# Attention, FFN and routed experts on one core: another order of the opening, and the first two tiles' mask laid into PSUM by TensorE

## The chip, the cores and the metric

The kernel runs on one core of a Trainium2 chip. The metric is the device time of one launch in microseconds (us). Engines: TensorE (PE), VectorE (DVE), ScalarE (ACT), GpSimd (POOL) and SyncE (SP), which issues most of the DMAs.

## The reference

Inputs are float32; two weight matrices of the FFN come as float64. Three stages follow each other:

```python
# 1: attention, batch 4, 8 heads, head_dim 64; 512 local and 32 global positions
k_all = np.concatenate([k_g, k_l], axis=2); v_all = np.concatenate([v_g, v_l], axis=2)
out_g = sm(scale * q_g @ k_all.T) @ v_all                  # global rows see all
mask = np.abs(pos[:, None] - pos[None, :]) <= 32           # local rows: a band, and the globals
s_ll = np.where(mask, scale * q_l @ k_l.T, -1000000000.0)
out_l = sm(np.concatenate([scale * q_l @ k_g.T, s_ll], -1)) @ np.concatenate([v_g, v_l], axis=2)
x = concatenate([out_g, out_l], axis=2)                    # as (4 * 544, 512) tokens
# 2: FFN 512 -> 2048 -> 512
h = x @ w_in; r = np.maximum(h, 0.0); x = (r * r) @ w_out
# 3: routed experts: 8 of 512 -> 1024 -> 512
do_compute = x @ w_skip > 0
e_idx = np.argmax(xc @ w_gate, axis=1)
out[do_compute] = xc + gate_w * (np.maximum(xc @ w1[e], 0.0) @ w2[e])
```

## The kernel before

Tokens are worked in 16 local tiles of 128 and one tile of globals; two tiles make a block of 256 for the FFN. Program order is fixed by hand (a manual schedule): each engine runs its instructions in the order in which the Python code emits them, and `SEQ`, a string of tokens that `do` (L1204 and after) walks through, sets that order up to the third FFN block. `EVEN`, `ODD` and `TAIL` do the same for the rest.

The tokens that matter here: `Lk..`, `Lq.`, `Lg.` issue loads of keys, queries and globals; `P00`, `P01`, `P0`, `P1` copy a loaded tile into the layout that the transposes want (L291, L310); `V` issues loads of the windows of values (`load_v`, L353); `W` fetches one weight of the FFN (L209), `A` takes one step of assembling weights (`assemble`, L237). `0G`, `00` to `03`, `0q` and `1q` transpose globals, keys and queries through PSUM and evict them (L316 to L343). `0a`, `0b`, `1a`, `1b` each advance the attention of tile 0, 1, 2 or 3 by one step, `F0`, `E0`, `H0`, `I0` the FFN of block 0 by one.

A weight arrives as float64, 128x512 numbers in 512 KB, and is turned into float32 by three kinds of steps: ACT rescales the high words (`rebase`, L219), DVE shifts the low words (`lower`, L223), joins the high words to them (`upper`, L227) and sets the sign (`sign`, L233). One `A` does `rebase` and `lower` of the next weight and `upper` and `sign` of this one; 32 weights are made so, in the order: four of w_in, four of w_out, and so on. Block 0 uses the first 24 of them as plain float32: its unit f needs the w_in weights 8*(f//4) to 8*(f//4)+3 for `first(f)` (h, L697) and one w_out weight for `second(f)` (acc, L723). Between them ACT takes the relu (g, L704) and ACT or DVE the square (gh, L743 or L741).

Attention of one tile (`attention`, L392) has six steps. (1) PE computes scores of 8 heads into two PSUM tiles, group 0 and 1 (L413); DVE adds the mask of group 0 (L426), takes the maximum (L430) and scales it (L431); ACT takes four exponents, one per head (L433). (2) The same for group 1. (3), (4) PE transposes the weights of a group (ptr, L442), ACT copies them to SBUF (pT, L444). (5) PE multiplies with the values (po, L451), DVE normalizes (xt, L461). (6) PE transposes the result (xtr, L280) and ACT copies it to the FFN's input (L468, `whole`). Transposes share two PSUM buffers, tag "tr", with group 1 of the scores of every tile but tile 1.

SP issues DMAs in the order of the code, each waiting for the one eight places ahead. Values lie in the opening in stages `v0` to `v3` (seven windows), later in six buffers `vr0` to `vr5`; each window is 96 local rows and, beneath them, the 32 global rows.

## Time and profile before

| | us |
|---|---|
| median of 3 runs (711.06 to 715.13) | 712.71 |
| the profiled execution | 706.99 |
| its span, first to last instruction | 705.3 |
| PE busy in the span | 680.9 (97%) |
| DVE / ACT / POOL busy | 395.0 / 365.2 / 163.9 |
| mean granted TensorE clock | 0.985 |

The profile is of one execution; the span is what its instructions cover, and 1.7 us lie around it. Busy shares are means over the whole program, so a stage is read in windows and in the timeline of each engine. In the timeline a row gives start, duration, engine, line, operation, what it writes and reads, shapes, the count of merged instructions, and in brackets how long the engine sat idle before it and what released it. The granted clock is a share of 2.4 GHz: 1.00 is 2.4 GHz, 0.50 is 1.2 GHz.

### The profile page before, as it was taken

How to read it: one execution, taken by the hardware profiler on the slowest of the kernel's cores; microseconds unless marked ns; L12 is line 12 of the kernel's file. 1: busy time of each engine (PE TensorE's matmuls, PEld its weight loads, DVE VectorE, ACT ScalarE, POOL GpSimd, SP SyncE). 2: the span in 40 equal slices, each digit the busy share in tenths (PEclk: the TensorE clock that was granted, in tenths of full speed). 3: DMA queues.
4: the chain of work that ended last, by engine and by line, in shares of the span. 5: the costliest groups of instructions: out<-in, count | busy, mean ns of one | idle time of the engine just before them, and what ended most of it. 6: DMA issues, size and time to landing. Idle time of an engine off the chain costs nothing. (4 is left out here: it accounts for less than half of the span.)

```text
span 705.3 us, 18628 instructions
## 1 busy us (share of the span) xinstructions
PE 680.9 (97%) x7621; PEld 573.8 (81%) x7621; DVE 395.0 (56%) x1072; ACT 365.2 (52%) x939; POOL 163.9 (23%) x206
## 2 busy tenths in 40 slices
PE   6689998999999999999999999999999999999996
PEld 4566667889888988888888998888887887898875
DVE  1889964872655165275426526544238733915985
ACT  5767568675535555453465445344434514614863
POOL 6000053453212212211211221122220432401311
PEclk8799999999999999999999999999999999999998
DMA  9999643064063401306340120410026689952930
GB/s 276 247 303 288 235 117 80 2 161 96 2 147 90 111 32 36 84 2 147 99 102 32 45 67 2 162 62 1 32 87 194 213 268 346 372 218 82 359 123 22
DMA packets 118841, 94.20 MB, mean 134 GB/s; under 512 B 84805, under 2 KB 91973, under 8 KB 118740
## 3 DMA queue, kind: packets, MB, share of 16 engines
q1 hardware_dynamic: 108352, 71.01, 35.9%
q10 hardware_dynamic: 8292, 15.48, 6.8%
q0 software_dynamic: 2096, 6.36, 2.7%
q8 instruction: 64, 1.05, 0.6%
q14 instruction: 37, 0.30, 0.2%
HBM read 80.57 MB, written 12.66 MB: 132 GB/s over the span
## 5 line engine op out<-in xcount | busy, mean ns | idle before, releaser
L184 POOL TENSOR_TENSOR gl<-g,gh 128x256 fp32r<-128x256 f32 x107 | 79.5, 743 | 302.8 <-ACT gh L183 142.3
L700 PE MATMUL h<-xh,w_in 128*128 128x256 f32 x464 | 135.1, 291 | 0.7 <-ACT xh L183 0.7
L701 PE MATMUL h<-xl,w_in 128*128 128x256 f32 x464 | 129.7, 280 | 0.3 <-DVE xl L184 0.3
L702 PE MATMUL h<-xh,w_in 128*128 128x256 f32 x464 | 129.8, 280 | 0.0
L725 PE MATMUL acc<-w_out,gh 128*128 128x512 f32 x232 | 97.6, 421 | 1.5 <-ACT gh L183 1.5
L727 PE MATMUL acc<-w_out,gl 128*128 128x512 f32 x232 | 91.9, 396 | 0.2
L726 PE MATMUL acc<-w_out,gh 128*128 128x512 f32 x232 | 91.7, 395 | 0.0
L700 PEld LDWEIGHTS h<-xh,w_in 128*128 128x128 f32 x464 | 87.2, 188 | 4.2 <-ACT xh L183 0.9
L701 PEld LDWEIGHTS h<-xl,w_in 128*128 128x128 f32 x464 | 87.3, 188 | 2.6 <-DVE xl L184 0.5
L704 ACT ACTIVATE g<-h 128x256 f32<-128x256 f32 x128 | 48.7, 381 | 77.0 <-PE h L702 43.7
L702 PEld LDWEIGHTS h<-xh,w_in 128*128 128x128 f32 x464 | 87.2, 188 | 0.0
L433 ACT ACTIVATE sm<-sm,mx 128x128 f32<-128x128 f32 x120 | 46.7, 390 | 49.5 <-DVE mx L431 49.5
L741 DVE TENSOR_TENSOR g<-h,g 128x256 f32<-128x256 f32 x53 | 22.2, 419 | 85.5 <-ACT g L704 85.5
L183 ACT CAST gh<-g 128x256 fp32r<-128x256 f32 x116 | 47.1, 406 | 42.2 <-DVE g L741 40.1
L727 PEld LDWEIGHTS acc<-w_out,gl 128*128 128x128 f32 x232 | 43.6, 188 | 11.9 <-POOL gl L184 1.3
L725 PEld LDWEIGHTS acc<-w_out,gh 128*128 128x128 f32 x232 | 43.6, 188 | 8.5 <-ACT gh L183 1.9
L726 PEld LDWEIGHTS acc<-w_out,gh 128*128 128x128 f32 x232 | 43.8, 189 | 5.7
L426 DVE TENSOR_TENSOR sm<-sc,mask 128x512 f32<-128x512 f32 x30 | 20.6, 687 | 23.3 <-PE sc L413 22.6
L255 POOL TENSOR_TENSOR w_in<-st_raw_in,w_in 128x512 fp32r<-128x512 f32 x10 | 13.0, 1308 | 80.0 <-ACT w_in L251 80.0
L743 ACT ACTIVATE g<-g 128x256 f32<-128x256 f32 x63 | 26.3, 417 | 5.0 <-ACT g L704 2.5
L413 PEld LDWEIGHTS sc<-kT,qT 64*32 64x32 f32 x2048 | 25.2, 110 | 4.3 <-issue 3.5
L413 PE MATMUL sc<-kT,qT 64*32 64x32 f32 (+1 forms) x2048 | 27.4, 230 | 0.0
(718 smaller groups left out, 1461.9 us busy)
## 6 DMA issues: line engine op xcount, KB each, us to landing
st_e<-in_moe_w_dram SPq DMA_DIRECT2D x46, 512.0 KB, 7.5
vr<-in_v_l_dram SPq DMA_DIRECT2D x49, 192.0 KB, 4.3
st_raw_in<-in_moe_w_in_dram SPq DMA_DIRECT2D x16, 512.0 KB, 6.6
st_raw_out<-in_moe_w_out_dram SPq DMA_DIRECT2D x16, 512.0 KB, 8.2
st_e<-in_moe_w_dram ACTq DMA_DIRECT2D x12, 512.0 KB, 5.5
x2d<-x ACTq DMA_DIRECT2D x19, 256.5 KB, 3.7
st_gv<-in_v_l_dram SPq DMA_DIRECT2D x8, 512.0 KB, 4.5
out_dram<-x ACTq DMA_DIRECT2D x16, 256.0 KB, 3.5
```

The lines of the kernel that those rows point to most:

```text
L183: nc.scalar.copy(hi, src)
L184: (lo_engine or nc.vector).tensor_tensor(out=lo, in0=src, in1=hi.bitcast(F32), op=ALU.subtract)
L413: nc.tensor.matmul(scs[g][SEG * i:SEG * (i + 1), p, cols], lhsT=q[rows, p, SEG * i:SEG * (i + 1)], rhs=kT[b][rows, p, keys], start=True, s ...
L433: nc.scalar.activation(sm[:, hh, :], sm[:, hh, :], AF.Exp, bias=mx[:, hh:hh + 1], scale=SCALE, accum_out=osum[:, 2 * hh + g:2 * hh + g + 1],)
L700: nc.tensor.matmul(h, lhsT=wh, rhs=xh[:, k, :], start=(k == 0), stop=False)
L701: nc.tensor.matmul(h, lhsT=wh, rhs=xl[:, k, :], start=False, stop=False)
L702: nc.tensor.matmul(h, lhsT=wl, rhs=xh[:, k, :], start=False, stop=(k == KD - 1))
L704: nc.scalar.activation(g, h, AF.Relu)
L725: nc.tensor.matmul(acc[z], lhsT=gh[:, c], rhs=wh, start=first_one, stop=False)
L726: nc.tensor.matmul(acc[z], lhsT=gh[:, c], rhs=wl, start=False, stop=False)
L727: nc.tensor.matmul(acc[z], lhsT=gl[:, c], rhs=wh, start=False, stop=last_one)
L743: nc.scalar.activation(square, g, AF.Square)
```

## The change

Five things. (1) `SEQ` has another beginning. (2) For tiles 0 and 1 TensorE lays the mask into the score tiles with one bf16 product per group (`ident_b`, an identity, is the stationary operand, and the mask, broadcast over four heads, the moving one), the scores accumulate upon it, DVE takes the maximum straight from PSUM, and ACT's exponents read PSUM; masks of all tiles are bf16 now. (3) One key copy, the evictions of key pairs 2 and 3, and half of the first query block's go from ACT to DVE. (4) The global rows of the values are loaded once; POOL copies them into the other six windows of the opening and into the six buffers of batch 0. (5) The load of the second query block comes later, two fetches of weights earlier.

```diff
 SEQ = """
-    Lk01 Lk00 P00 Lg0 0G P01 Lq0 P0 00 02 V Lq1 01 0q W 03 W A W W 0a A V V 0a A W W A 0a 0b 0a 0b A 0b W P1 W 0a A
-    0b A V 0a W 0b V A 1q W W A 0b V 1a W W F0 A W E0 1a W W A W V 1a A F0 W 1a I0 A 1b L9 1a H0 V A A W V E0 W 1a
+    Lk01 Lk00 P00 Lg0 0G P01 Lq0 P0 00 02 W W V 01 0q W W 03 A 0a V 0a A Lq1 0a 0a A V W 0b 0b V 0a W A W P1 0a 0b
+    0b W A W V 0b 0b W V 1q W F0 A 1a W A E0 A 1a A W V F0 A 1a W W I0 A 1a A 1b W W W L9 1a H0 V A A A W V E0 W 1a
     X0 H0 A A E0 H0 W H0 A H0 W 1b E0 Lg1 A A W W A E0 1b W H0 A 1b E0 A H0 A E0 Lv00 A W W W 1g A I0 C 1b A 1g I0 W
...
-        m = const.tile([P, P], F32, name=f"mask{kind}")
+        m = const.tile([P, P], BF16, name=f"mask{kind}")
...
+    ident_b = const.tile([P, P], BF16, name="ident_b")
+    nc.gpsimd.tensor_copy(ident_b, ident)
...
-            puts[f"{b}{z}"] = lambda: nc.scalar.copy(kin[b, z], t.rearrange("p h j d -> p j h d"))
+            copy = nc.vector.tensor_copy if z else nc.scalar.copy
+            puts[f"{b}{z}"] = lambda: copy(kin[b, z], t.rearrange("p h j d -> p j h d"))
...
-        nc.scalar.copy(kT[b][:, p, 0:SL].rearrange("p (q j) -> p j q", j=TPB), tr)
+        copy = nc.vector.tensor_copy if b == 0 and p > 1 else nc.scalar.copy
+        copy(kT[b][:, p, 0:SL].rearrange("p (q j) -> p j q", j=TPB), tr)
...
-                nc.scalar.copy(qT[j][:, 2 * z + a, :].rearrange("p (q i) -> p i q", i=2), tr[:, a])
+                copy = nc.vector.tensor_copy if j == 0 and z else nc.scalar.copy
+                copy(qT[j][:, 2 * z + a, :].rearrange("p (q i) -> p i q", i=2), tr[:, a])
...
+                if len(opening) == 1:
+                    nc.sync.dma_start(heads(w[WIN:P]), v_g[b].rearrange("h s d -> s h d"))
+                else:
+                    nc.gpsimd.tensor_copy(w[WIN:P], opening[0][WIN:P])
                 nc.sync.dma_start(heads(w[0:WIN]), v_l[b, :, w0:w0 + WIN, :].rearrange("h s d -> s h d"))
-                nc.sync.dma_start(heads(w[WIN:P]), v_g[b].rearrange("h s d -> s h d"))
...
-                nc.sync.dma_start(heads(windows[k][WIN:P]), v_g[b].rearrange("h s d -> s h d"))
+                if b == 0:
+                    nc.gpsimd.tensor_copy(windows[k][WIN:P], opening[-1][WIN:P])
+                else:
+                    nc.sync.dma_start(heads(windows[k][WIN:P]), v_g[b].rearrange("h s d -> s h d"))
...
+        masked = t < 2
+        if masked:
+            for sc in scs:
+                nc.tensor.matmul(
+                    sc, lhsT=ident_b, rhs=mask.unsqueeze(1).to_broadcast([P, 4, P]), start=True, stop=False,
+                )
...
-                            start=True, stop=True,
+                            start=not masked, stop=not masked or (globals_ and p == NPAIR - 1),
...
-            nc.vector.tensor_tensor(
-                out=sm, in0=scs[g], in1=mask.unsqueeze(1).to_broadcast([P, 4, P]), op=ALU.add,
-            )
+            if masked:
+                src = scs[g]
+            else:
+                src = sm
+                nc.vector.tensor_tensor(
+                    out=sm, in0=scs[g], in1=mask.unsqueeze(1).to_broadcast([P, 4, P]), op=ALU.add,
+                )
             mx = sb("mx", 2, [P, 4], f"mx{t}_{g}")
-            nc.vector.tensor_reduce(out=mx, in_=sm, op=ALU.max, axis=AX.X)
+            nc.vector.tensor_reduce(out=mx, in_=src, op=ALU.max, axis=AX.X)
...
-                    sm[:, hh, :], sm[:, hh, :], AF.Exp, bias=mx[:, hh:hh + 1], scale=SCALE,
+                    sm[:, hh, :], src[:, hh, :], AF.Exp, bias=mx[:, hh:hh + 1], scale=SCALE,
```

Lines of the changed program lie a few to 21 further down: the scores are L430 there, the mask's product L420, maximum and scaling L451 and L452, exponents L454.

What that does to the order is seen best on three engines. A name such as sm1_0 is of tile 1, group 0; the last number is the buffer's. First DVE, from the scores of tile 0 on, before:

```order
L426 TENSOR_TENSOR sm0_0_339<-sc0_0_273,mask0_75 128x512
L430 TENSOR_REDUCE mx0_0_341<-sm0_0_339 128x4
L431 TENSOR_SCALAR mx0_0_341<-mx0_0_341 128x4
L227 SCALAR_TENSOR_TENSOR st_raw_in_0_0_256<-st_raw_in_0_0_256 128x512
L223 TENSOR_SCALAR st_raw_in_1_0_264<-st_raw_in_1_0_264 128x512
L233 SCALAR_TENSOR_TENSOR st_raw_in_0_0_256<-st_raw_in_0_0_256 128x512
L426 TENSOR_TENSOR sm0_1_362<-sc0_1_274,mask0_75 128x512
L430 TENSOR_REDUCE mx0_1_364<-sm0_1_362 128x4
L431 TENSOR_SCALAR mx0_1_364<-mx0_1_364 128x4
```

and now, from the same place:

```order
L451 TENSOR_REDUCE mx0_0_341<-sc0_0_272 128x4
L452 TENSOR_SCALAR mx0_0_341<-mx0_0_341 128x4
L451 TENSOR_REDUCE mx0_1_354<-sc0_1_273 128x4
L452 TENSOR_SCALAR mx0_1_354<-mx0_1_354 128x4
L229 SCALAR_TENSOR_TENSOR st_raw_in_0_0_231<-st_raw_in_0_0_231 128x512
L225 TENSOR_SCALAR st_raw_in_1_0_233<-st_raw_in_1_0_233 128x512
L235 SCALAR_TENSOR_TENSOR st_raw_in_0_0_231<-st_raw_in_0_0_231 128x512
L229 SCALAR_TENSOR_TENSOR st_raw_in_1_0_233<-st_raw_in_1_0_233 128x512
L225 TENSOR_SCALAR st_raw_in_2_0_259<-st_raw_in_2_0_259 128x512
```

Between tile 0's two maxima no weight step stands any more, and the adds are gone; the weight steps come behind.

Second PE, around tile 1's scores (po is the product with the values). Before, behind the scores:

```order
L413 MATMUL sc1_1_392<-kT0_198,qT0_241 32x32
L442 MATMUL ptr0_1_466<-ident_70,sm0_1_362 128x128 x4
L442 MATMUL ptr1_0_485<-ident_70,st_sm1_457 128x128 x4
L451 MATMUL po0_497<-st_v0_229,pT0_0_388 32x64 x3
L451 MATMUL po0_497<-st_v1_354,pT0_0_388 32x64
```

and now, ahead of them:

```order
L463 MATMUL ptr0_0_368<-ident_70,sm0_0_340 128x128 x4
L463 MATMUL ptr0_1_375<-ident_70,sm0_1_353 128x128 x4
L420 LDWEIGHTS ident_b_153
L420 MATMUL sc1_0_394<-mask1_101,ident_b_153 128x512
L420 LDWEIGHTS ident_b_153
L420 MATMUL sc1_1_395<-mask1_101,ident_b_153 128x512
```

Both transposes of tile 0 stand ahead of tile 1's mask and scores now; one stood behind.

Third ACT, around the first unit of block 0's FFN (g0_0, gh0_0; st_raw are weight steps, sm2_0 is tile 2). Before:

```order
L219 ACTIVATE st_raw_in_0_1_561<-st_raw_in_0_1_561 128x512
L468 COPY st_x0_559<-xtr1_633 128x4x128
L433 ACTIVATE sm2_0_714,osum2_647<-sm2_0_714,mx2_0_716 128x128 x4
L704 ACTIVATE g0_0_732<-h0_0_727 128x256
L219 ACTIVATE st_raw_in_1_1_625<-st_raw_in_1_1_625 128x512
L743 ACTIVATE gh0_0_740<-g0_0_732 128x256
L704 ACTIVATE g0_1_747<-h0_1_742 128x256
```

and now:

```order
L489 COPY st_x0_533<-xtr1_600 128x4x128
L348 COPY qT1_616<-qtr1_0_617 128x2x128 x2
L348 COPY qT1_616<-qtr1_1_624 128x2x128 x2
L725 ACTIVATE g0_0_638<-h0_0_633 128x256
L221 ACTIVATE st_raw_out_1_519<-st_raw_out_1_519 128x512
L454 ACTIVATE sm2_0_711,osum2_644<-sm2_0_711,mx2_0_713 128x128 x4
L221 ACTIVATE st_raw_out_2_525<-st_raw_out_2_525 128x512
L764 ACTIVATE gh0_0_726<-g0_0_638 128x256
```

The query evictions of tiles 2 and 3 and the weight steps stand elsewhere; tile 2's exponents stand ahead of gh0_0 in both, with the relu g0_0 ahead of them now.

## Rows read from the trace of the kernel before

**Rows 1.** Windows: stretch, length, busy us of each engine, granted clock, DMA share, GB/s.
```profile
0.00:45.00 45.00, 31.81 (x607) 22.55 (x608) 27.85 (x59) 29.21 (x83) 10.76 (x46) 0.81 1.03 264
...
45.00:80.00 35.00, 35.00 (x387) 23.96 (x386) 31.46 (x64) 23.01 (x61) 0.00 (x0) 1.00 1.04 320
```

**Rows 2.** Timeline of PE: start, duration, line, operation, count, idle before.
```profile
1.45 3.60 PE L1255 MATMUL warm<-idle 128*128 128x512 bf16 x8 [1.45 <-DVE idle L1250]
...
14.36 2.04 PE L413 MATMUL sc<-kT,qT 64*32 64x96 f32 x128
...
18.77 1.64 PE L442 MATMUL ptr<-ident,sm 128*128 128x128 f32 x4 [2.37 <-ACT sm L433]
...
20.34 2.38 PE L413 MATMUL sc<-kT,qT 64*32 64x96 f32 x128
...
27.25 1.63 PE L442 MATMUL ptr<-ident,st_sm 128*128 128x128 f32 x4 [3.94 <-ACT st_sm L433]
...
36.42 1.62 PE L413 MATMUL sc<-kT,qT 64*32 64x96 f32 x128
...
37.98 3.51 PE L697 MATMUL h<-st_x,st_raw_in 128*128 128x256 f32 x15
...
42.99 0.49 PE L697 MATMUL h<-st_x,st_raw_in 128*128 128x256 f32 x1 [1.50 <-issue]
...
43.32 0.60 PE L442 MATMUL ptr<-ident,sm 128*128 128x128 f32 x4
...
43.76 1.97 PE L723 MATMUL acc<-st_raw_out,gh 128*128 128x512 f32 x4
...
71.70 1.89 PE L697 MATMUL h<-st_x,st_raw_in 128*128 128x256 f32 x8
```

**Rows 3.** Windows again, around two holes of PE and behind them.
```profile
20.00:22.00 2.00, 2.00 (x99) 1.51 (x99) 1.93 (x5) 1.16 (x5) 0.00 (x0) 0.50 0.60 125
...
26.00:32.00 6.00, 4.75 (x74) 3.52 (x75) 5.08 (x12) 5.30 (x21) 0.00 (x0) 0.50 1.03 261
...
33.00:45.00 12.00, 9.58 (x221) 7.68 (x217) 11.62 (x25) 7.85 (x28) 0.00 (x0) 1.00 1.12 263
```

**Rows 4.** Timeline of DVE.
```profile
16.57 0.69 DVE L426 TENSOR_TENSOR sm<-sc,mask 128x512 f32<-128x512 f32 x1 [2.73 <-PE sc L413]
...
25.06 0.68 DVE L426 TENSOR_TENSOR st_sm<-sc,mask 128x512 f32<-128x512 f32 x1
...
38.71 0.68 DVE L426 TENSOR_TENSOR sm<-sc,mask 128x512 f32<-128x512 f32 x1
...
57.82 0.69 DVE L227 SCALAR_TENSOR_TENSOR st_raw_out<-st_raw_out 128x512 int32<-128x512 int32 x1
...
59.36 0.69 DVE L227 SCALAR_TENSOR_TENSOR st_raw_out<-st_raw_out 128x512 int32<-128x512 int32 x1
...
69.13 0.69 DVE L233 SCALAR_TENSOR_TENSOR st_raw_in<-st_raw_in 128x512 int32<-128x512 int32 x1
...
82.20 0.67 DVE L507 COPY gpT<-gptr 128x512 f32<-128x512 f32 x1
...
83.32 1.13 DVE L227 SCALAR_TENSOR_TENSOR st_raw_in<-st_raw_in 128x512 int32<-128x512 int32 x1
```

**Rows 5.** Timeline of ACT.
```profile
14.47 1.09 ACT L331 COPY kT<-ktr 128x512 f32<-128x512 f32 x1 [0.21 <-PE ktr L330]
...
18.22 0.40 ACT L433 ACTIVATE sm<-sm,mx 128x128 f32<-128x128 f32 x1 [2.19 <-DVE mx L431]
...
42.17 0.65 ACT L219 ACTIVATE st_raw_in<-st_raw_in 128x512 f32<-128x512 f32 x1
...
42.72 0.40 ACT L743 ACTIVATE gh<-g 128x256 f32<-128x256 f32 x1
```

**Rows 6.** Timeline of POOL.
```profile
12.48 1.03 POOL L310 COPY st_q<-st_q_in 128x1024 f32<-128x1024 f32 x1
...
82.60 1.30 POOL L255 TENSOR_TENSOR w_in<-st_raw_in,w_in 128x512 fp32r<-128x512 f32 x1 [69.10 <-ACT w_in L251]
```

## The prediction

> **What bounds the kernel now.** I read the windows first. From 45 to 80 us the PE is busy in all 35 of 35 us; in the first 45 us in 31.81 of 45, so the opening is where time can be had: 13.2 us of idle PE, and part of the rest at half clock [rows 1]. In the second row VectorE (DVE) is busy 31.46 of 35 us as well: behind a full PE stands a nearly full DVE, which puts the float64 weights together. The reader should keep that in mind, because this change moves DVE's work about.
>
> Then the timeline of PE, for the holes. Tile 0's scores end at 16.4, and PE next works at 18.77 (2.37 us idle); tile 1's scores run 20.34 to 22.7, but ptr1_0 comes only at 27.25 (3.94 us idle); the first FFN product starts at 37.98, and its first second-layer product, acc, at 43.76 [rows 2]. Third the granted clock: 0.50 at 20 to 22 and at 26 to 32 us, that is 1.2 GHz, behind each of the two holes, and 1.00 (2.4 GHz) all through 33 to 45, although PE had a hole of 1.50 us ahead of 42.99 there [rows 2, 3]. So holes of 2.4 and 3.9 us were followed by the low clock, one of 1.5 was not. Last DVE and ACT, for what ended the holes: ACT's exponents start at 18.22, right behind DVE's add and maximum of 16.57, and DVE reaches tile 1's add only at 25.06, 2.4 us after PE had its scores ready, since weight steps stand in front [rows 2, 4, 5].
>
> All times below are of the profiled execution (706.99 us, span 705.3); the median of the three runs is 712.71, 0.8% higher. I work out a difference and apply it to the median. About 0.5% (3.6 us) is what a measurement of this kernel can tell from no change.
>
> **The change part by part.**
>
> *Evictions shared.* ACT loses one 128x1024 copy, two key evictions and one query eviction to DVE. A strided key eviction costs ACT 1.09 us [rows 5]; DVE's copy out of PSUM of that size takes 0.67 [rows 4]. If all of that came off the path, scores would start 1 us sooner; but the transposes alternate over the two "tr" buffers, and the chain ktr0_0, ktr0_1, qtr0_0, ktr0_3 runs over one eviction after the other as before. Walking it, ktr0_3's transposes end at 14.4, as now. Bounds 13.4 and 14.4; I take 14.4, because only one of the four evictions in that chain (the last) got cheaper.
>
> *Mask by TensorE.* Four bf16 products of 128x512 come in, and four DVE adds of 0.69 go out, 2.75 us of DVE. The nearest row for a product is the warm-up's: 8 in 3.60 us, 0.45 each [rows 2]; half of that at the high clock. Tile 0 pays two at the low clock, 0.9 us, between 14.4 and its scores, which then end at 17.0 instead of 16.4 (the wait for the last key eviction in there is gone). From the end of the scores to the first exponent DVE now needs 1.8 us (16.4 to 18.22), of which the add's 0.69 goes: 17.0 + 1.1, the first exponents start at 18.1, level with 18.22 [rows 2, 4, 5]. Group 1 needs no second add and no weight step in front: its exponents end at 21.2 instead of 22.8. The exponents read PSUM instead of SBUF; nothing there has a row, so I take them at 0.40 as now [rows 5].
>
> *The new order.* PE now does ptr0_0 and ptr0_1 ahead of tile 1's scores, so it starts at 18.6 with ptr0_0 (a hole of 1.5 us, where it had 2.37), waits for group 1 until 21.35, then lays the mask (0.44) and scores (1.62 at full clock, as the row of 36.42 [rows 2]): scores of tile 1 end at 24.1, which is later than 22.7. But DVE stands ready: two maxima, exponents end at 28.2 instead of 30.2. Weighted values, xtr, pT copies, po1, xtr1 and the query transposes follow on PE and ACT at the durations of before, and the first FFN product starts at 33.8 instead of 37.98. Of these 4.2 us, 1.6 are no gain: tile 2's scores stood in front of it and now stand behind.
>
> Next late is gh0_0. On ACT it is queued behind tile 2's four exponents and one more weight step, both before and after. Tile 2's scores end at 37.15, then the same 1.8 to the first exponent, four exponents of 0.40, a weight step of 0.55 (42.17 to 42.72) and gh's 0.40: acc starts at 41.5 instead of 43.76 [rows 2, 5]. ptr2_0, 0.44, was ahead of it and is now behind [rows 2]. **Lead at the first acc: 43.76 - 0.44 - 41.5 = 1.8 us.** Just ahead of it PE is idle from 39.0 to 41.5.
>
> *The weights.* Each weight costs DVE 1.54 us (57.82 to 59.36 [rows 4]). Ahead of the first FFN product five assemblies remain of nine, so afterwards there are 15 up to weight 19, whose signs end at 69.8 now (69.13 + 0.69), and which h0_8 needs at 71.70 [rows 2, 4]: a slack of 1.9 us only. From tile 2's add at 38.71 to 69.8 it does 12 of them and all else that stands there, 31.1 us. After the change this add comes at 37.25, and 15 assemblies are left instead of 12, 4.6 us more: 37.25 + 31.1 + 4.6 = 73.0. What it can win back are its own waits, 3.5 us of 35 between 45 and 80 [rows 1], say 3 of these 31: 70.0. DVE thus ends between 70.0 and 73.0, no earlier than before although its work shrank by 2.75: it stands idle from about 33.4 to 37.25 waiting for tile 2's scores, since the weights that filled that place were put behind.
>
> PE's own way from acc to h0_8 is 28.4 us long (71.70 - 43.76 + 0.44): 69.9, and three small new waits (an estimate: 0.35 for tile 2's ptr2_1, 0.35 for its pT, 0.5 for its xt, each being queued behind one weight step more on ACT or DVE) make it 71.1 against 71.70. **Sum: 0.6 us earlier.** From there on both programs have one order, and PE is the bound.
>
> *Values copied on chip.* Twelve small loads leave SP's queue and 13 copies of 32x512 go to POOL; a POOL copy of twice that length took 1.03 us [rows 6], so 0.5 each, between 12 and 24 us. The query block q1 moves behind six loads on SP, its copy on POOL behind seven copies; it is needed at 33. The weights come forward; no engine waited for them but at the start. I cost this part at nothing: the cover is DVE's and POOL's idle time before 25 us. Without that cover: at 83.32 DVE needed 1.13 us for a step that takes 0.69, while POOL worked from 82.60 to 83.90 [rows 4, 6]. The Trainium skill (GPSIMD Engine Reference, Key points) says that POOL shares its SBUF interfaces with VectorE and contends with DVE's two-input instructions. This rule speaks against the change; by it, and 6.5 us of copies all beside weight steps, an estimate would be some 2.5 us more on DVE instead of nothing.
>
> **The rivals.**
>
> *Faster.* The lead of the first FFN product survives whole, because gh0_0 and the weights wait less than I count: 37.98 - 33.8 - 1.6 = 2.6 us, and up to 3.9 with the start of the scores at 13.4 and cheaper exponents. For: 13.2 us of holes are there to be had. Against: a slack of 1.9 us at h0_8. It gives 710.1, down to 708.8.
>
> *Slower: DVE becomes the bound of the weights.* Place: h0_8 (and h0_4 before it, which needs weight 11). Ten assemblies instead of six lie between the first FFN product and the split of tile 0's x. Price: DVE at 73.0 makes h0_8 1.3 us late; with DVE slowed beside POOL as at 83.32, or ACT's weight steps later than I have them (ACT gets four more in that stretch too), up to 3. It decides as soon as weight 19's signs end behind 71.7. It gives 714.3, from 714.0 to 715.7. For it: DVE busy 31.46 of 35 [rows 1].
>
> *The clock.* The hole ahead of the first acc is 2.5 us, longer than the 2.37 that a low clock followed. The stretches at 0.50 in rows 3 cover 2 to 6 us; at half clock PE loses 1 to 3 us there, less the 1.2 us of waits that PE has anyway, plus my -0.6: 713.3, to 714.5.
>
> **How the numbers follow.** Forecast 0.45: 712.71 - 0.6 = 712.1, a time that no measurement tells from 712.7; alone it spans 711 to 713.3. Faster rival 0.22, DVE 0.20, clock 0.13. Over 0.5% faster means below 709.1: most of the faster rival's far end and what I overlook, 0.17. Over 0.5% slower means above 716.3: the two slower rivals together, 0.12. Within: 0.71. The range goes from the faster rival's far end, 708.8, to the DVE rival's, 715.7.
>
> **What would show it.** Right: scores of tile 0 end near 17.0 and the exponents of group 1 near 21.2; the first FFN product near 34; a hole of about 2.5 us ahead of the first acc, at 41.5; weight 19 done near 71 and h0_8 within 1 us of 71.1; the clock at 1.00 from 33 on. Wrong: a first FFN product after 36 (then the PE order costs what the maxima save); h0_4 or h0_8 waiting for DVE; the clock at 0.50 after 41.5; h0_8 before 69.5, which would mean that DVE never gated.

## The result, and the profile after

The changed kernel takes 715.74 us (median of 12 runs, 714.41 to 716.79), the kernel before beside it 710.27 (12 runs, 708.5 to 715.13): a ratio of 1.0072 [1.0059, 1.0085], 5.1 us slower by that ratio (the two medians differ by 5.5). The forecast was 0.6 us faster. The profiled execution has a span of 714.5 us against 705.3; that of before (706.99 us) lies 3.3 us below its median, so the spans differ by more than the medians do.

Timeline of PE in the changed kernel, columns as in [rows 2]:

```profile
15.61 2.05 PE L430 MATMUL sc<-kT,qT 64*32 64x96 f32 x128
19.26 1.52 PE L463 MATMUL ptr<-ident,sm 128*128 128x128 f32 x4 [1.60 <-ACT sm L454]
...
22.61 1.06 PE L420 MATMUL sc<-mask,ident_b 128*128 128x512 bf16 x2
23.60 2.37 PE L430 MATMUL sc<-kT,qT 64*32 64x96 f32 x128
25.90 1.29 PE L472 MATMUL po<-st_v,pT 128*32 128x64 f32 x40
30.41 0.78 PE L472 MATMUL po<-st_v,pT 128*32 128x64 f32 x24 [3.22 <-issue]
...
39.60 1.90 PE L718 MATMUL h<-st_x,st_raw_in 128*128 128x256 f32 x8
...
45.96 0.92 PE L718 MATMUL h<-st_x,st_raw_in 128*128 128x256 f32 x3 [1.63 <-issue]
47.42 3.61 PE L744 MATMUL acc<-st_raw_out,gh 128*128 128x512 f32 x4 [0.53 <-ACT gh L764]
...
78.37 1.89 PE L718 MATMUL h<-st_x,st_raw_in 128*128 128x256 f32 x8
...
81.98 1.06 PE L506 MATMUL gsa<-kT,qgT 64*32 64x512 f32 x8
```

Against [rows 2] tile 0's scores end 1.26 us late (17.66), the first FFN product (39.60) is 1.62 late, the first acc (47.42) 3.66, h0_8 (78.37) 6.67. The global scores, gsa, begin at 81.98 where before had 75.32; from there on the lag stays near 7 us up to 600. So 6.7 of the 9.3 us between the two spans are lost ahead of 82 us. Another 1.5 come at 605, among the experts, where PE waits for DVE as it did not in before, and 0.8 behind PE's last product:

```profile
605.17 0.41 PE L1195 MATMUL ertr_rest_a<-ident,er_rest_a 128*128 128x128 f32 x2 [1.69 <-DVE eg_rest_a L1197]
```

A loss of 1.4 to 1.9 us arises there in the traces of experiments 3 and 12 too and in no other, whatever their opening; it is left aside here, and what comes ahead of 82 is studied.

Two rows carry the case: tile 0's products with the values, po, stop after 40 of their 64 passes, and the second FFN unit, h0_1, stops after five of eight, both "<-issue": PE waited for nothing that the profile shows. At that place of po the program has no wait either; its waits stand at po's first, third and fourth product and at the first of group 1. The kernel before has one such row ahead of 60 us, 1.50 at 42.99 [rows 2].

Windows of the changed kernel, columns as in [rows 1] (the granted clock is the third number from the end, the DMA share the second):

```profile
21.00:27.00 6.00, 5.30 (x174) 4.29 (x174) 3.56 (x6) 2.86 (x8) 5.39 (x7) 0.50 1.13 272
...
31.00:38.00 7.00, 5.42 (x86) 4.43 (x79) 5.03 (x11) 2.33 (x4) 0.00 (x0) 0.54 1.22 232
38.00:47.00 9.00, 7.02 (x156) 5.43 (x154) 4.34 (x9) 4.93 (x17) 0.00 (x0) 1.00 1.09 315
48.00:51.00 3.00, 3.00 (x5) 1.06 (x4) 2.93 (x7) 0.92 (x5) 0.00 (x0) 0.50 0.94 319
```

The clock is at 0.50 (1.2 GHz) behind the holes of 1.60 and 0.92 us ahead of tile 0's two weight transposes, behind the halt in po, and behind the halt in h0_1, where the first acc takes 3.61 us instead of 1.97. DMA shares are near or above 1 all through: the queues are full of loads.

Timeline of DVE in the changed kernel:

```profile
22.25 0.84 DVE L229 SCALAR_TENSOR_TENSOR st_raw_in<-st_raw_in 128x512 int32<-128x512 int32 x1 [1.27 <-ACT st_raw_in L221]
23.01 0.84 DVE L225 TENSOR_SCALAR st_raw_in<-st_raw_in 128x512 int32<-128x512 int32 x1
23.77 1.09 DVE L235 SCALAR_TENSOR_TENSOR st_raw_in<-st_raw_in 128x512 int32<-128x512 int32 x1
26.02 0.69 DVE L451 TENSOR_REDUCE mx<-sc 128x4 f32<-128x512 f32 x1 [1.16 <-PE sc L430]
```

DVE, the engine that I feared would bind, waits for ACT and PE here.

### The profile page after: what moved, and what is told of

Its sections match the earlier page's. It is cut to its first block, busy times and chain, and to the rows that moved or that the text cites. A ratio compares the mean times of both kernels' runs of the same rounds, so it can differ in the third digit from the quotient of the medians.

```text
span 714.5 us, 18645 instructions
## 1 busy us (share of the span) xinstructions
PE 686.2 (96%) x7625; PEld 576.4 (81%) x7625; DVE 397.3 (56%) x1073; ACT 360.7 (50%) x934; POOL 171.3 (24%) x219
## 3 DMA queue, kind: packets, MB, share of 16 engines
q8 instruction: 64, 1.05, 0.6%
## 5 line engine op out<-in xcount | busy, mean ns | idle before, releaser
L454 ACT ACTIVATE sm<-sm,mx 128x128 f32<-128x128 f32 x112 | 43.6, 391 | 50.7 <-DVE mx L452 50.7
L447 DVE TENSOR_TENSOR sm<-sc,mask 128x512 f32<-128x512 f32 x28 | 19.3, 688 | 24.3 <-PE sc L430 23.5
L430 PEld LDWEIGHTS sc<-kT,qT 64*32 64x32 f32 x2048 | 25.4, 110 | 4.8 <-issue 4.0
L430 PE MATMUL sc<-kT,qT 64*32 64x32 f32 (+1 forms) x2048 | 27.2, 231 | 0.0
```

Source lines behind the costliest of these rows:

```text
L430: nc.tensor.matmul(scs[g][SEG * i:SEG * (i + 1), p, cols], lhsT=q[rows, p, SEG * i:SEG * (i + 1)], rhs=kT[b][rows, p, keys], start=not mas ...
L454: nc.scalar.activation(sm[:, hh, :], src[:, hh, :], AF.Exp, bias=mx[:, hh:hh + 1], scale=SCALE, accum_out=osum[:, 2 * hh + g:2 * hh + g + 1],)
```

## What the halts are: a count and a packet

Count PE's rows from the start, two instructions for each pass (a weight load and a product). In every trace of this study the halts put down to "issue" ahead of 58 us then lie within four of 442, 698, 946 or 1200, whatever stands there: in before at 1198, here at 696 and 1202. With PE's instructions that only wait counted too, the places are 449 or 450, 705 or 706, 961 or 962, and 1217 or 1218: 256 apart. And a little ahead of the end of each lies one packet of the queue "instruction". The view of the DMA queues of the changed kernel (queue, kind: packets, MB, share of 16 engines) has, for 27.75 to 28.00 us,

```profile
q8 instruction: 1, 0.02, 26.9%
```

and po goes on at 30.41. **Theory: PE's instructions come in parts of 256, one packet each, through the DMA engines that also carry the data; the next part is asked for when one is begun, and groups of small products use a part up before the next has come.** Here the part begun at about 24.3 (23.60 and 80/256 of the 2.37 us of tile 1's scores) was used up under 3 us later, and the next was usable at 30.41, 6.1 us after its predecessor was begun. In before, the 3.94 us for which PE waited for tile 1's exponents [rows 2] lay in between. **Rivals:** po waits for data (a load of values or one of POOL's copies); the low clock is what costs; DVE's weights bind.

## The experiments

All ratios are to the kernel before on the same chip. Kernels that are alike up to there differ by 1 to 2 us in where tile 0's scores end (17.66 in the change, 16.65, 16.51 and 15.65 in experiments 5, 7 and 9, whose edits act later), so stretches are counted from there; a table of them stands in the section after this one. Where an edit adds or takes away products ahead of that point (3, 4, 6, 8, 11, and the mask of the change against before), it moves the origin too, and such a count is less sure.

**1. The order alone**, put into the kernel before:

```diff
-    ... P00 Lg0 0G P01 Lq0 P0 00 02 V Lq1 01 0q W 03 W A W W 0a A V V 0a A W W A 0a 0b 0a 0b A 0b W P1 W 0a A
+    ... P00 Lg0 0G P01 Lq0 P0 00 02 W W V 01 0q W W 03 A 0a V 0a A Lq1 0a 0a A V W 0b 0b V 0a W A W P1 0a 0b
... (and the line behind it, as in the change)
```

> The kernel before with the new SEQ and none of the other parts: masks added by DVE, all evictions on ACT, global values loaded by SP. Theory O (the order is what costs: tile 1's scores and the product po0 now follow each other on PE with no pause, and PE then stands for instructions, 3.22 us at 27.2 in the changed kernel, where no wait stands in the program): slower than before, ratio 1.005 to 1.015, with a PE idle of 2 us or more inside po0 that has no releaser. Theory P (the parts cost: POOL's copies, the mask's products, DVE's evictions): within 0.3% of before, 0.997 to 1.003, no such idle.

Measured: 1.0047 [1.0031, 1.0063], 712.86 against 709.25. PE's timeline has the halt, after 694 instructions:

```profile
27.61 0.53 PE L451 MATMUL po<-st_v,pT 128*32 128x64 f32 x21 [2.29 <-issue]
```

This kernel has no copies by POOL, and its values are loaded as in before. The order by itself brings 0.47 of the 0.72%, just under the 0.5 to 1.5 expected, and the larger part of the loss as far as the intervals can tell.

**2. The order undone**: the changed kernel with the old first lines of `SEQ`.

```diff
-    ... P00 Lg0 0G P01 Lq0 P0 00 02 W W V 01 0q W W 03 A 0a V 0a A Lq1 0a 0a A V W 0b 0b V 0a W A W P1 0a 0b
+    ... P00 Lg0 0G P01 Lq0 P0 00 02 V Lq1 01 0q W 03 W A W W 0a A V V 0a A W W A 0a 0b 0a 0b A 0b W P1 W 0a A
... (and the line behind it, as in before)
```

> The changed kernel with the old SEQ: mask in PSUM, shared evictions, values copied on chip, old order. Theory O: within 0.4% of before, 0.994 to 1.002, and no idle inside po0. Theory P: 1.004 to 1.008, most of the loss of 0.72% stays.

Measured: 1.0012 [0.9999, 1.0024]. No halt in po; it stands now in tile 2's scores, at 944, and a short one at 1198:

```profile
39.50 1.44 PE L430 MATMUL sc<-kT,qT 64*32 64x96 f32 x116 [2.32 <-issue]
...
45.81 1.24 PE L718 MATMUL h<-st_x,st_raw_in 128*128 128x256 f32 x5 [0.68 <-issue]
```

Mask products, shared evictions and copied values together cost or bring nothing that is measured.

**3. The count shifted**: the changed kernel with 154 more PE instructions at the start, which nothing uses.

```diff
-WARM = 8
+WARM = 5
...
+            for _ in range(80):
+                nc.tensor.matmul(o[0:SEG, 0:SEG], lhsT=idle[0:D, 0:SEG], rhs=idle[0:D, 0:SEG], start=True, stop=True)
```

> The changed kernel with its 8 warm-up products replaced by 5 of them and 80 very small ones (64x32 by 64x32, bf16, 160 more PE instructions), which moves every later instruction of PE 154 places on in its stream and computes nothing else. Theory O in the form that PE runs out of fetched instructions (one packet of 16 KB on the instruction queue at 27 to 29 us, in the middle of the stall): the idle inside po0 goes from 3.22 us to under 0.5, the first FFN product starts 2.5 to 3.5 us sooner than 39.6, the ratio falls from 1.0072 to about 1.003. A rival, that po0 waits for data (a window of values, POOL's copy) or for a resource that the profile does not show: the idle stays at 3 us at the same product, the ratio stays at 1.007.

Measured: 1.0197 [1.0172, 1.0221], of five runs; 1.003 was expected. The halt has left tile 0's po and stands inside the scores of tile 0 and of tile 1, at 442 and 698:

```profile
20.79 0.44 PE L430 MATMUL sc<-kT,qT 64*32 64x96 f32 x26 [3.95 <-issue]
...
30.50 0.52 PE L430 MATMUL sc<-kT,qT 64*32 64x32 f32 x36 [1.54 <-issue]
```

A product in the middle of the scores waits for no data. The halt belongs to a place in the stream of instructions, not to an operation: the rival that po waits for data falls. I did not foresee that the part from 442 would be so late; its packet lies at 18.24 us, and the first packet begins between 17.3 and 19.3 in all traces. Two shorter halts stand later in this trace, 1.18 at 59.19 (after 1708 instructions) and 1.55 at 605.12.

**4. The mask alone**, in the kernel before (bf16 masks, the four products, the maxima and exponents from PSUM, as in the change).

```diff
+        if masked:
+            for sc in scs:
+                nc.tensor.matmul(
+                    sc, lhsT=ident_b, rhs=mask.unsqueeze(1).to_broadcast([P, 4, P]), start=True, stop=False,
+                )
```

> The kernel before with the mask of tiles 0 and 1 laid by TensorE, and nothing else changed. Theory O: between 0.996 and 1.002; 2.75 us of DVE work go, tile 0's scores end some 0.6 to 1.2 us later because of two products at 0.53 us. Theory P, if the mask's products or exponents from PSUM are what costs: 1.003 or more.

Measured: 1.0004 [0.9983, 1.0025]; halts of 0.50 at 442 and 1.41 at 1198. PE also waits in tile 1's po for loads of the values' global rows:

```profile
32.09 0.27 PE L464 MATMUL po<-st_v,pT 128*32 128x64 f32 x2 [1.30 <-DMA st_v<-in_v_g_dram]
33.96 1.89 PE L464 MATMUL po<-st_v,pT 128*32 128x64 f32 x58 [1.59 <-DMA st_v<-in_v_g_dram]
```

That these waits are what keeps DVE's saving from showing is argued, not shown.

**5. A wait over the fetch**: the changed kernel with po behind tile 1's first weight transposes.

```diff
-    ... 0b 0b V 0a W A W P1 0a 0b 0b W A W V 0b 0b ...
+    ... 0b 0b V W A W P1 0b 0a 0b 0a W A W V 0b 0b ...
```

> The changed kernel with one step of tile 0 (the products with the values, po0) moved behind the first transposes of tile 1's weights, which wait for tile 1's exponents. Theory (PE runs out of fetched instructions when two groups of small products follow each other; counted from the start the stalls lie 256 instructions apart, and the next part is usable 4.5 to 6.5 us after the part before it was begun): the stall in po0 falls from 3.2 us to under 1, since PE waits there anyway; the first FFN product starts 1.5 to 2.5 us before 39.6; the whole lies 1 to 2.5 us below the change, at a ratio of 1.003 to 1.006. Rival (po0 waits for data, a copy of POOL or a load of values, that comes at about 30.4): po0, started later, shows no stall, but everything behind it comes no sooner, and the ratio stays at 1.007.

Measured: 1.0045 [1.0029, 1.0061].

```profile
35.31 1.90 PE L718 MATMUL h<-st_x,st_raw_in 128*128 128x256 f32 x8
...
44.84 1.62 PE L718 MATMUL h<-st_x,st_raw_in 128*128 128x256 f32 x4 [4.38 <-issue]
46.25 3.05 PE L744 MATMUL acc<-st_raw_out,gh 128*128 128x512 f32 x4
```

The halt in po is gone. Counted from the end of tile 0's scores (16.65 here) the first FFN product comes 3.3 us sooner than in the change, more than I expected, but the first acc only 0.2, because the halt at 1200 grew from 1.63 to 4.38. **The lead won in front of one fetch is lost here at the fetch behind it.**

**6. The clock kept up**: experiment 5 with the eight warm-up products put into two holes, so that the count of instructions stays.

```diff
+    ... A 0a V 0a A Lq1 K3 0a 0a A V W 0b 0b V W A W P1 K5 0b 0a
-WARM = 8
+WARM = 0
...
+            if what[0] == "K":
+                for _ in range(int(what[1:])):
+                    nc.tensor.matmul(
+                        junk, lhsT=ones, rhs=ones.unsqueeze(1).to_broadcast([P, 4, P]), start=True, stop=True
+                    )
```

> The kernel of the experiment before, with TensorE's eight warm-up products of bf16 taken away from the start and put into two holes: three ahead of tile 0's first weight transposes, five ahead of tile 1's. The number of PE instructions ahead of po0 stays the same. Theory that the low granted clock behind the holes (0.50 at 21 to 27 and 31 to 38 us in the change) costs PE time on the path: the clock stays at 1.00 through a part of 18 to 38 us, the first FFN product comes 1 to 2 us sooner than in the experiment before, the whole 1 to 2 us sooner. Rival (behind the holes the path runs over ACT and DVE, so PE's clock costs nothing there): first FFN product and time within 0.5 us and 0.1% of the experiment before.

Measured: 1.0035 [1.0009, 1.006], not to be told from experiment 5. The windows show the clock at 1.00 from 18 to 38 us:

```profile
18.00:30.00 12.00, 7.76 (x198) 4.38 (x199) 10.30 (x19) 8.70 (x38) 6.16 (x7) 1.00 1.15 300
30.00:38.00 8.00, 6.60 (x156) 5.29 (x150) 4.75 (x10) 4.18 (x11) 0.00 (x0) 1.00 1.21 234
```

The first FFN product comes at 35.75, no sooner than the 35.31 of experiment 5; the halt at 1200 is 4.08, and one of 0.89 is back in po. Counted from tile 0's scores, which end 1.05 us later here, it comes 0.6 us sooner, and the first acc 1.3. So the low clock ahead of 38 us is not the main cost, and whether it costs up to 1 us is not settled: the time does not tell.

**7. Quiet queues at the first halt**: the changed kernel with one tiny transfer on SP that waits for tile 1's maxima, ahead of the sixth weight, so that SP issues no weight from 18.3 to 27.0 us. (The expectation miscounts it as the seventh.)

```diff
-    ... 0b 0b V 0a W A W P1 0a 0b
+    ... 0b 0b V Y 0a W A W P1 0a 0b
...
+            if what == "Y":
+                nc.sync.dma_start(gate, maxima[-1])
```

> The changed kernel with one tiny transfer put into SP's queue ahead of the seventh weight, which waits for tile 1's maxima (26.7 us); so no weight load is issued from about 20 to 27 us, and the DMA queues run empty there. Theory (the fetch of PE's instructions is late because it stands behind the data loads): the instruction packet that now lies at 27.75 us comes before 26, and the stall in po0 shrinks from 3.2 to below 1.5 us; later the weights are late by up to 3 us on DVE. Rival (the fetch takes its time whatever else the queues carry): packet at 27.5 to 28 and stall of about 3 us as in the change.

Measured: 1.0027 [1.0006, 1.0048]. The DMA share falls to 0.05 at 24 to 26 us, the instruction packet lies in 23.50 to 23.75, as the share falls, instead of 27.75 to 28.00, and the halt in po is 0.84 instead of 3.22:

```profile
23.00:23.50 0.50, 0.50 (x49) 0.50 (x35) 0.50 (x1) 0.00 (x0) 0.50 (x2) 0.50 1.29 191
...
24.00:26.00 2.00, 1.35 (x91) 1.15 (x75) 1.31 (x3) 0.31 (x2) 1.56 (x3) 0.98 0.05 10
```

```profile
q8 instruction: 1, 0.02, 31.9%
```

```profile
26.20 0.54 PE L475 MATMUL po<-st_v,pT 128*32 128x64 f32 x24 [0.84 <-issue]
...
42.84 1.65 PE L721 MATMUL h<-st_x,st_raw_in 128*128 128x256 f32 x3 [3.72 <-issue]
44.28 3.62 PE L747 MATMUL acc<-st_raw_out,gh 128*128 128x512 f32 x4
```

From the start of the part at about 23.1 (22.41 and 80/256 of 2.15) to the next one's first instruction it is 3.1 us, with full queues 6.1. **The fetch of this part was late because of the data loads.** The halt at 1202, with the queues full again, is 3.72 us, and the first acc behind it runs at half clock.

**8. The clock kept up in the kernel before**, with its eight warm-up products put into its hole of 3.94 us.

```diff
-    ... W W A 0a 0b 0a 0b A 0b W P1
+    ... W W A 0a 0b 0a 0b A K8 0b W P1
-WARM = 8
+WARM = 0
```

> The kernel before, with the eight warm-up products taken from the start and put into the hole of 3.94 us ahead of tile 1's first weight transposes, so that the number of PE instructions behind them is unchanged. Theory that the low clock behind this hole (0.50 at 26 to 32 us) costs time: clock at 1.00 from 27 on, first FFN product at 36.5 to 37 instead of 37.98, and the stall of 1.50 ahead of the second FFN unit ends 1 us sooner as well; ratio 0.997 to 0.999. Rival (the path there runs over ACT and DVE): no change, 1.000.

Measured: 0.9988 [0.9969, 1.0006], inconclusive as a time. The clock is at 1.00 from 26 to 32 us, as meant, but tile 1's po then waits 0.72 and 0.88 us for the global rows of the values, the first FFN product comes at 39.66, and the halt at 1198 is 2.49 where it was 1.50. Neither 36.5 to 37 nor an earlier end of the halt came; this execution lies 2.2 us above the median of its kernel, so its stretches say little against before's.

**9. Quiet queues at both halts**: as 7 (`Y0`), and a second gate, `Y1`, which waits for the relu of the first FFN unit, ahead of the ninth weight.

```diff
-    ... 0b 0b V 0a W A W P1 0a 0b 0b W A W V 0b 0b W V 1q W F0 A 1a W A E0 ...
+    ... 0b 0b V Y0 0a W A W P1 0a 0b 0b W A V 0b 0b V 1q F0 Y1 W W W A 1a W A E0 ...
```

> The changed kernel with two tiny transfers in SP's queue: the seventh weight's load and what follows waits for tile 1's maxima, the ninth's and what follows for the relu of the first FFN unit. So the DMA queues run nearly empty at about 24 to 27 and at 34 to 38 us, where PE begins the parts of its instructions behind which it stalled. Theory (what the new order costs is PE's instruction fetch behind the data loads): stalls in po0 below 1.2 us and in the second FFN unit below 1.5 us (1.63 in the change, 3.72 with the first gate alone), first acc at 41.5 to 43 instead of 47.42, clock at 1.00 behind it, whole 4 to 9 us under the change, that is at a ratio of 0.994 to 1.002. Rival (DVE's weights bound the stretch from 45 to 80 us): the first acc comes early but global scores at 75.3 or later as in the kernel before, ratio 1.002 to 1.005; waits for DVE or for weights stand ahead of PE between 45 and 75.

Measured: **1.0011 [0.9995, 1.0028]**, 711.39 against 710.25. The window at the second gate, and PE's timeline:

```profile
34.00:38.00 4.00, 3.82 (x140) 3.38 (x140) 0.33 (x1) 2.34 (x7) 0.00 (x0) 1.00 0.59 101
```

```profile
26.28 0.54 PE L475 MATMUL po<-st_v,pT 128*32 128x64 f32 x24 [1.10 <-issue]
...
34.68 1.90 PE L721 MATMUL h<-st_x,st_raw_in 128*128 128x256 f32 x8
...
38.06 2.00 PE L721 MATMUL h<-st_x,st_raw_in 128*128 128x256 f32 x8
42.49 2.07 PE L748 MATMUL acc<-st_raw_out,gh 128*128 128x512 f32 x4 [2.43 <-ACT gh L768]
...
48.64 1.61 PE L432 MATMUL sc<-kT,qT 64*32 64x96 f32 x126 [0.96 <-ACT pT L468]
...
73.47 1.89 PE L721 MATMUL h<-st_x,st_raw_in 128*128 128x256 f32 x8
...
77.08 1.06 PE L509 MATMUL gsa<-kT,qgT 64*32 64x512 f32 x8
```

h0_1 runs through, and the first acc runs at full clock. With the order, the mask, the evictions and the copies all kept, only the loads held off, 1.0072 becomes 1.0011: holding them off gives back 4.3 of the 5.1 us (0.0061 of 710; by the two intervals this is sure to some 1.5 us), while the halts go from 3.22 and 1.63 to 1.10 and none and the half clock behind the second goes with it. This execution began 2.0 us ahead of the change's (tile 0's scores end at 15.65), before a gate acts, so of its 4.9 us at the first acc 2.9 are the gates'. The rival's picture is true in part: at the first acc it stands 0.5 us ahead of before, so counted, and at gsa 2.5 behind. PE waits 0.96 for tile 2's pT and 0.23 twice for gh; the view of waits names none of PE's products for DVE or for weights between 45 and 75 us (one weight load of PE waits 0.2 for xt).

**10. One gate in the kernel before**, ahead of the weights around its first FFN unit.

```diff
-    ... A 1q W W A 0b V 1a W W F0 A W E0 ...
+    ... A 1q A 0b V 1a F0 Y1 W W W W A W E0 ...
```

> The kernel before with one such gate: the weights that it fetches around the first FFN unit wait for the relu of that unit, so that few loads are in flight at 36 to 39 us. Theory: its own stall ahead of the second FFN unit (1.50 us, ending at 42.99) shrinks below 0.7; but the first acc gains less than 1 us, since the square of the first unit comes at about 43 on ACT; ratio 0.998 to 1.000. Rival (the stall is no matter of the loads): 1.5 us as before, ratio 1.000 to 1.003 from weights that come later.

Measured: 1.006 [1.0038, 1.0082]; the ratio was missed. Its halt of 1.50 us is gone, as the theory has it, but ACT waits for a held-off weight, and the first square, the first acc's input, stands behind that step:

```profile
46.54 0.70 ACT L221 ACTIVATE st_raw_in<-st_raw_in 128x512 f32<-128x512 f32 x1 [4.57 <-DMA st_raw_in<-in_moe_w_in_dram]
```

The first acc comes at 47.58. A gate must not hold a load whose user stands ahead of the path.

**11. Two gates, and the clock kept up** (four and three of the warm-up products in the holes ahead of tile 0's weight transposes).

```diff
-    ... A 0a V 0a A Lq1 0a 0a A V W 0b 0b V Y0
+    ... A 0a V 0a A Lq1 K4 0a K3 0a A V W 0b 0b V Y0
-WARM = 8
+WARM = 1
```

> The kernel with two gates, and seven of the eight warm-up products put into the two holes that the new order leaves ahead of tile 0's weight transposes (four and three). If the low clock at 20 to 24 us costs time on the path there, the scores of tile 1 end 0.5 to 1 us sooner and so does all behind, 0.1% under the kernel with two gates; rival (that stretch is followed by a wait for ACT or for fetched instructions anyway): the same within 0.1%.

Measured: 1.0011 [0.9994, 1.0029], the same as experiment 9. Tile 1's scores end 0.9 us sooner (23.15 against 24.02), and the halt in po takes it: 2.34 for 1.10, with po going on at 26.32 against 26.28. Counted from tile 0's scores, which end 0.8 us later here, a lead of 0.8 to 0.9 is left up to gsa; whether that is the clock or the execution is not shown.

**12. All of it**: two gates, po behind ptr1_0, fifteen more products in the holes, and the second FFN unit with the first square ahead of tile 2's scores.

```diff
+    ... A 0a V 0a A Lq1 K4 0a K3 0a A V W 0b 0b V Y0 W A W P1 K8 0b 0a
+    0b 0a W A V 0b 0b V 1q F0 Y1 W W W W A A E0 1a A 1a A W V F0
```

> What the runs so far say, put together: the kernel with two gates, with po0 behind tile 1's first weight transposes (a wait that covers the fetch), fifteen more bf16 products in three holes of PE (clock, and the boundary of 256 instructions moved off the first acc), and the second FFN unit and the square of the first, with two weight assemblies, ahead of tile 2's scores, since with two gates the first acc waited 2.43 us for that square, queued behind tile 2's exponents. Expected: no stall over 0.6 us in po0, first FFN product at 32.5 to 34 (34.68 with two gates), first acc at 38 to 40 (42.49), global scores at 73.5 to 75.5 (77.08; 75.32 before), ratio 0.995 to 0.999. Rival (DVE's weights and tile 2's chain bound the stretch behind): the first acc is as early, but PE waits 2 us and more for pT, xt or weights between 42 and 75, global scores at 76 or later, ratio 1.000 to 1.002.

Measured: 1.0001 [0.9984, 1.0018], 709.82 against 709.86.

```profile
38.09 2.06 PE L748 MATMUL acc<-st_raw_out,gh 128*128 128x512 f32 x4
...
46.31 1.61 PE L432 MATMUL sc<-kT,qT 64*32 64x96 f32 x126 [0.97 <-ACT pT L468]
...
74.77 1.06 PE L509 MATMUL gsa<-kT,qgT 64*32 64x512 f32 x8
```

No halt is left ahead of gsa (one of 1.24 stands at 604.23); the first acc is 5.7 us ahead of before, and gsa only 0.55. Tile 2's weight transposes now come before all of their inputs are there (1.48 and 1.49 us each where they take 0.60), and PE waits for pT and gh behind them. This is in part the rival of the expectation: the lead is given back behind the first acc, about 4 of the 5 us in tile 2's chain and at gh (waits of PE of 0.37, 0.97, 0.29 and 0.21, 1.8 in stretched transposes, 0.4 of a transpose that in before stood ahead of the acc); the rest was not taken apart. No version was found that beats the kernel before by more than its interval.

## Why the prediction was wrong

The step that failed is the sentence of the new order that weighted values, xtr, po1 and the rest "follow on PE and ACT at the durations of before", together with a clock of 1.00 from 33 on. It priced PE's work, its waits for other engines and its clock, and had no term for PE being without instructions, although [rows 2] hold such a row (1.50, "<-issue"), which I had read only as a hole that no low clock followed. Measured in its place: halts of 3.22 us in tile 0's po and of 1.63 in h0_1, and 1.64 us for the first acc at half clock. That 715.74 lies so near the end of the range, 715.7, is luck: the base of three runs, 712.71, was 2.4 us above the 710.27 of twelve, and the greatest loss that any rival priced was 3.0 us, where 5.1 were measured.

The stretches from the end of tile 0's scores, in us, each from one execution:

| | first FFN product | first acc | gsa | ratio |
|---|---|---|---|---|
| before | 21.6 | 27.4 | 58.9 | 1 |
| forecast | 16.8 | 24.5 | 57.7 | 0.9992 |
| the change | 21.9 | 29.8 | 64.3 | 1.0072 |
| 1, order alone | 21.1 | 29.3 | 63.9 | 1.0047 |
| 2, order undone | 23.3 | 29.7 | 61.1 | 1.0012 |
| 3, count shifted | 20.5 | 28.3 | 63.1 | 1.0197 |
| 4, mask alone | 23.4 | 29.1 | 60.6 | 1.0004 |
| 5, po behind ptr1_0 | 18.7 | 29.6 | 62.5 | 1.0045 |
| 6, as 5, clock up | 18.1 | 28.3 | 61.1 | 1.0035 |
| 7, one gate | 17.9 | 27.8 | 61.3 | 1.0027 |
| 8, before, clock up | 23.8 | 30.6 | 62.1 | 0.9988 |
| 9, two gates | 19.0 | 26.8 | 61.4 | 1.0011 |
| 10, before, one gate | 22.6 | 32.0 | 65.7 | 1.006 |
| 11, two gates, clock up | 18.2 | 26.0 | 60.5 | 1.0011 |
| 12, all | 16.7 | 21.8 | 58.4 | 1.0001 |

(The forecast's gsa is its h0_8 plus the 3.62 us from there to gsa in before.) Among the kernels with the new order (the change, 1, 5 to 7, 9, 11, 12) the column of gsa falls with the ratio, within 0.3 us: what is won or lost by then is most of the result. Experiment 3 does not fit, since a halt of 3.95 stands inside its tile 0's scores, ahead of the origin, and 8 does not. The executions differ too: that of before lies 3.3 us below its kernel's median, that of 9 2.5 below, that of 8 2.2 above. The first FFN product comes as early as foretold only in experiment 12, where no halt is left and the clock is kept up.

Point by point:

- *Evictions.* Tile 0's scores end at 17.66, foretold 17.0. DVE's key eviction takes 1.10 us, not the 0.67 of a copy that is not strided, hence no cheaper than ACT's 1.09; the two mask products 0.53 each, not 0.45. That is 0.7 us in all in this execution; kernels alike up to there ended them at 15.65 to 16.65, so the sum of this part is not shown to be wrong.
- *Mask.* Right: first exponents 1.08 us behind the scores (18.74), where I had 1.1; exponents from PSUM take 0.36 to 0.40; group 1's end at 21.55, foretold 21.2. By itself the part is worth nothing that can be measured (experiment 4).
- *The new order, up to tile 1.* Its scores end at 25.97, foretold 24.1. 1.4 of it is the half clock (mask 1.06 for 0.44, scores 2.37 for 1.62) behind holes of 1.60 and 0.92 us. I had one hole of 1.5 in the trace that no low clock followed, and took that for these.
- *First FFN product.* 21.9 us behind tile 0's scores, foretold 16.8. Of the missing 5.1 the halt is 3.22 and the late scores of tile 1 are 1.2 (8.3 behind tile 0's, foretold 7.1); the clock is at 0.54 from 31 to 38 where the other 0.7 arises. The 16.7 of experiment 12, in another order and with added products, speaks for the durations themselves.
- *Hole and first acc.* The hole of 2.5 us ahead of the acc is there in experiment 9, 2.43 us, for gh, which is late for the reason given (behind tile 2's exponents). In the change the halt at 1202 stands in that place, and the acc behind it runs at half clock, 1.64 us more.
- *Three small waits.* Foretold 1.2 us, measured 1.42 in experiment 9 (0.96, 0.23, 0.23). That the sum is near is luck: of the three places only pT is among them, with 0.96 for 0.35; the other two waits are for gh, where I had none, and the products of ptr2_1 and xt wait for nothing.
- *The clock.* The rival had the place (behind the hole ahead of the first acc) and the size, 1 to 3 us, but another cause of the hole. Its own times do not follow from its terms: 1 to 3 us, less 1.2, less 0.6, on 712.71 is 711.9 to 713.9, not 713.3 to 714.5. In the stretch up to 38 us the low clock costs nothing that the times can tell (experiments 6 and 11).
- *DVE as the bound.* Wrong: no row of PE up to gsa waits for a weight, and DVE itself waits. *Copies by POOL at nothing.* Right as far as these rows show: there are 12 of them and not 13, they take 0.62 to 0.75 us each, not 0.5, and the three weight steps beside them from 22.25 on take 2.77 us where such steps take 1.80 elsewhere; behind them DVE waits 1.16 us for tile 1's scores. The Trainium skill (GPSIMD Engine Reference, Key points) says that POOL shares its SBUF interfaces with VectorE and contends with instructions that have two SBUF inputs or run in a 2-port perf mode. The trace agrees on the two-input steps (0.84 and 1.09 for 0.69). A one-input step was stretched as well (0.84 for 0.42); whether it ran in such a mode no run here shows.

With the halts cut to one of 1.10 us the change is what was forecast, no difference that can be measured (1.0011 [0.9995, 1.0028]), though 0.8 us to the slow side where I had 0.6 to the fast; this rest was not taken apart. The three small waits are in it, and the trace of experiment 9 has gsa later than the forecast by more than they make up (61.4 for 57.7).

## What to carry to other kernels

Where PE runs through some hundreds of small products without a pause, look for rows "<-issue" and count the instructions to them: if they are evenly spaced and a packet of instructions lies ahead of each, the fetch of instructions is a resource like any other, and a wait that an order removes may have been its cover. Before a wait is taken away, ask what was fetched under it; and hold off bulk loads that are not needed yet, but never one whose user stands ahead of the path. Here that brought the change back level with before, not ahead of it.

## What was not expected of the hardware

- PE halts at places that lie 256 instructions apart. In the halts ahead of 58 us that stand behind full data queues, the part behind such a place was usable 4.5 to 9.7 us after the one ahead of it was begun (6.1 in the change's po; the first halt of experiment 3 aside), and 3.1, 4.0 and 4.3 us in the po of experiments 7, 9 and 11, where a gate had let the queues run empty. From the quarter of a microsecond that holds the packet to the first instruction behind it, it is 2.6 to 3.1 us in every one of these halts, with full queues and with empty ones (27.75 and 30.41; 23.50 and 26.20; 42.25 and 44.84; in before 40.00 and 42.99). So what the loads delay is the packet, not what comes behind it.
- The page of the changed kernel counts 64 packets and 1.05 MB in that queue: 16 KB each, and 64 times 256 is 16384, somewhat above the 15250 weight loads and products that the trace has for PE.
- Open: the first of these packets begins at 17.3 to 19.3 us in all traces, whatever PE had done by then (experiment 3), and what sets that was not tried. When a part is asked for is inferred: from the second on, the packets ahead of 58 us begin 0.4 to 7.2 us behind the start of the part before, and twice 1.0 us ahead of it (experiments 9 and 11). Full queues do not make every fetch late: in experiment 1 the part begun at 39.8 was followed by the next at 42.9 without a halt, at a DMA share near 1.
- Open: the late halts. Those at 605.12 (experiment 3) and 604.23 (experiment 12, among products of 128x512) end 2.6 and 2.7 us behind a packet, as the early ones do; one of 0.42 at 211.77 in experiment 11 does not. In the change DVE's copy for which PE waits at 605 begins 2.7 us behind a packet of 8 KB of another instruction queue, q14 (at 601.85); whether DVE stood there for its own instructions was not tried.
